# Attention and two gated layers on one core: side pieces stored one slot after their join, the last ones moved beside the fourth layer, and the third matrix's low parts on GpSimd

## The chip, the cores and the metric

The kernel runs on one core of a Trainium2 chip. The metric is the device time of one execution in microseconds. Five engines run their own queues in order and meet only at semaphores: TensorE (PE, with its weight loads as PEld), VectorE (DVE), ScalarE (ACT), GpSimd (POOL) and SyncE (SP), which here only issues DMAs. ACT issues DMAs too. An instruction that waits holds everything behind it on its engine's queue.

## What is computed

```python
def reference(**kwargs):
    attn_out = _attn_ref(q, k, v, w_pre, w_post)          # 4 batches, 12 heads, 448 positions, 64 per head
    x = attn_out.transpose(0, 2, 1, 3).reshape(1792, 768)
    x = ((x @ w1) * (x @ w2) @ w3) @ w_out                # moe:  768 -> 1024 -> 1024 -> 768
    h = np.maximum(x @ w_in, 0.0)                         # moe2: 768 -> 2048
    return h * h @ w_out2                                 # 2048 -> 768
```

Everything is float32. The change touches only what comes after the attention.

## The kernel before

**Numbers in two parts.** A float32 matrix is split into a high part (rounded by ACT, `high`, L120) and a low part (what is left, `rest`, L148), and each product is three matmuls, high by high, low by high and high by low (`mm3`, L56). PE therefore needs, for each weight piece, first `wh` and, from its third matmul on, `wl`. Some weights come from memory as eight-byte words. Such a piece is loaded by SP, folded by ACT (`fold`, L93), put together by DVE in two steps (the join, L104 and L106) and then split.

**Units and slots.** The class `Moe` lists units of work: `l1` (first layer), `p34` (the product w3 by w_out, made once, so that third and output matrix become one), `ly` (that product's layer, 12 slots for the first half of the tokens), `l3_quad` (the layer with w_in, seven block products `qh..A` to `qh..D` instead of eight, which need sums `Sh` of weight blocks), and `l4_part`. `run` goes over the units slot by slot. For each slot `stage` first writes the preparation of later pieces (load six ahead, fold four ahead, join and `high` three ahead, `rest` two ahead), and then the slot's matmuls and what becomes of their results. This program order is the order on every engine.

In the program, a `p34` slot has 24 matmuls of 384 columns, an `ly` slot 24 matmuls of 448 columns, a slot of a quad nine of 448, and an `l4` slot 24 of 448. An `ly` slot leaves one block of y. `yquad` (L891) evacuates it on ACT, rounds it, and, on every fourth slot (block B22), makes the differences T2, T3 and T4 on DVE, whose high parts ACT makes and whose low parts POOL makes (DVE for the last column).

**Side pieces.** The matrix w_in comes as eight-byte words too. It is put together ahead of its use in 32 side pieces, which are written back to the scratch tensor `wind` and read from there by the quads. `side(k)` (L967) handles at step k the join of piece k-2 (fold on ACT at L93, two DVE steps at L974 and L975), its store on ACT's queue (L978), and the load of piece k on SP (L981). The load reuses the buffer of piece k-2, so SP waits for that join. The condition at L671 says which slots have a step: both slots of each `p34` unit, one of two in the four `l1` units behind it, then all slots from `ly` on until 32 pieces are through. The last loads stand in the last `ly` slots, and the last two joins in the first two slots of the first quad.

**Low parts of the third matrix.** The pieces of `p34` carry a third field (L956). `stage` takes that as the sign to put their `rest` on DVE (L609). Other pieces' low parts are on POOL.

Of the kernel before, what the change touches and what calls it, by code (L numbers as in the profile page):

```python
# [26 lines left out]
PW = 512  # L27
# [10 lines left out]
def fused_kernel(ctx, tc, q, k, v, w_pre, w_post, w1, w2, w3t, wo, win, wo2, eye, out):  # L38
    nc = tc.nc
    PSUM = bass.MemoryType.PSUM  # L40

    def pool(stack, name, side="left", space=None):
        kw = {"space": space} if space is not None else {}
        return stack.enter_context(tc.tile_pool(name=name, bufs=1, side=side, reuse_waits="tile", **kw))
# [5 lines left out]
    wind = dram.tile([16, 128, DM], F, name="wind")  # L50
# [5 lines left out]
    def mm3(acc, terms, first=True, last=True, again=False):  # L56
        n = len(terms)
        for i, ((wh, wl), (xh, xl)) in enumerate(terms):
            for j, (w, x) in enumerate(((wh, xh), (wh, xl), (wl, xh))):
                nc.tensor.matmul(  # L60
                    acc, w, x, start=(first and i == 0 and j == 0), stop=(last and i == n - 1 and j == 2),
                    skip_group_check=again,
                )

    class Weights:


        def __init__(self, p, pre, wo, nraw, ny, nf, nhi, nlo):
            self.pre = pre
            self.p, self.wo, self.nraw, self.ny, self.nf, self.nhi, self.nlo = p, wo, nraw, ny, nf, nhi, nlo  # L70
            self.raw, self.yt, self.ft, self.out = {}, {}, {}, {}
# [461 lines left out]
    class Moe:  # L533
        def __init__(self, pre):
            self.w = Weights(None, pre, PW, 4, 2, 3, 8, 8)
            self.wp, self.pre = None, pre
            self.xy, self.late, self.acc, self.ready = {}, [[] for _ in range(8)], {}, set()
            self.units, self.wot = [], {}
            self.sides = 0
            for hf in range(2):  # L540
                if hf == 0:
                    l1 = [self.l1(hf, m, s) for m in range(6) for s in range(2)]
                else:
                    l1 = [self.l1_quad(j, s) for j in range(4) for s in range(2)]
                if hf == 0:

                    wop = [self.wo_piece(c, h) for c in range(8) for h in range(2)]
                    mixed, rest = l1[:4] + wop[:6], wop[6:]
                    for i in range(8):
                        mixed.append(l1[4 + i])  # L550
                        for _ in range(1 + (i % 4 == 3)):
                            mixed.append(rest.pop(0))
                    assert not rest
                    l1 = mixed
                self.units += l1
                ly = [self.ly(hf, n) for n in range(6)]
                if hf == 0:
                    self.p34_at = len(self.units)
                    self.units += [self.p34(m) for m in range(8)]
                    self.units += [self.l1(0, m, x) for m in (6, 7) for x in range(2)]  # L560
                self.turned = len(self.units)
                self.units += [self.ly(hf, n) for n in range(6)]
                for gr in range(4):
                    js = ((0, 1, 2), (3, 4), (5, 6, 7) if hf == 0 else (5, 6), () if hf == 0 else (7,))[gr]
                    self.units += [self.l3_quad(hf, j) for j in js]
                    es = [(0, 1), (2,), (3,), (4,), (5,)] if hf and gr == 3 else [(e,) for e in range(6)]
                    self.units += [self.l4_part(hf, gr, x) for x in es]
            kept = [u[2] if len(u) > 2 else None for u in self.units]
            self.units = [u[:2] for u in self.units]
            self.pieces = [s for ss, _ in self.units for s in ss]  # L570
            n = np.cumsum([0] + [len(ss) for ss, _ in self.units])
            self.at = [int(x) for x in n]
            self.keep = {
                self.at[i] + j: u[0][:, u[1] * j : u[1] * j + u[1]]
                for i, u in enumerate(kept) if u for j in range(len(self.units[i][0]))
            }
# [83 lines left out]
        def run(self, ps):  # L660
            self.ps = ps
            order = [None, None, (0, 1), None, (1, 1), None, (2, 1), None, (3, 1)]
            for i in range(10, len(self.units)):
                one = [(i, t) if self.units[i][1] else None for t in range(len(self.units[i][0]))]
                order += one[::-1] if i == self.turned else one
            for p, it in enumerate(order):
                def go():
                    i, t = it
                    ws = [self.w.out.get(self.at[i] + j) for j in range(len(self.units[i][0]))]
                    self.units[i][1](ws, t)  # L670
                    if i >= self.p34_at and (t or not self.p34_at + 8 <= i < self.p34_at + 12):  # L671
                        self.side(self.sides)
                        self.sides += 1

                self.stage(p + 5, go if it else None)

# [269 lines left out]
        def p34(self, m):  # L946
            def run(ws, t):
                acc = self.psum(f"p34_{m}_{t}")[:, :HC]
                mm3(acc, [(self.chunk(ws, c), self.wot[c, t]) for c in range(8)])
                o = self.tile(f"o34_{m}_{t}")[:, :HC]  # L950
                nc.scalar.activation(o, acc, AF.Copy)
                nc.scalar.dma_start(
                    w34d[3 * t : 3 * t + 3, :, m].rearrange("n p c -> p n c"), o.rearrange("p (n c) -> p n c", c=128)
                )

            return [(w3t[m, :, PW * i : PW * i + PW], True, None) for i in range(2)], run  # L956

        def ly(self, hf, n):
            def run(ws, t):
# [7 lines left out]
        def side(self, k):  # L967
            part = lambda x, i: x[i // 2, :, HC * (i % 2) : HC * (i % 2) + HC]
            if 0 <= k - 2 < 32:
                raw = self.w.raw["side", k - 2]  # L970
                f = self.tile(f"side{k - 2}")[:, :HC]
                fi = f.bitcast(I32)
                self.w.fold(raw[:, :, 1].bitcast(F), ("side", k - 2))
                nc.vector.tensor_scalar(fi, raw[:, :, 1], 3, None, ALU.logical_shift_left)  # L974
                nc.vector.scalar_tensor_tensor(  # L975
                    fi, raw[:, :, 0], 29, fi, ALU.logical_shift_right, ALU.bitwise_or
                )
                nc.scalar.dma_start(part(wind, k - 2), f)  # L978
            if 0 <= k < 32:
                t = self.w.raw["side", k] = self.ap.tile([128, HC, 2], I32, tag="sraw", name=f"sraw{k}", bufs=2)  # L980
                nc.sync.dma_start(t.rearrange("p n t -> p (n t)"), part(win, k).bitcast(I32))  # L981
# [152 lines left out]
```

## Time and profile before

| | |
|---|---|
| median of 3 runs | 1301.47 us (1301.25 to 1303.01) |
| the profiled execution's own time | 1300.55 us |
| its span, first to last instruction | 1298.4 us |
| granted TensorE clock, mean over the span | 0.996 |
| busy: PE, DVE, ACT, POOL | 97%, 69%, 58%, 45% of the span |

The profile has one row for a group of instructions or for one instruction, with its start, its duration and, in square brackets, how long its engine was idle before it and what ended that. PE's durations overlap, since matmuls are pipelined: what counts for it is the distance from one start to the next. Shares over the whole span are averages over stages with different limits, so the stretches of the stages around the change are read apart.

### The profile page before, as it was taken

What the parts mean: (1) busy time and instruction counts of PE and PEld (TensorE: products, weight loads), DVE (VectorE), ACT (ScalarE), POOL (GpSimd) and SP (SyncE); (2) the same over time, 40 slices, a digit from 0 to 9 for tenths busy, and PEclk for the clock granted to TensorE, in tenths of its full rate; (3) what the DMA queues carried; (4) which work ended last, traced back from release to release, by engine and by line L of the source; (5) the groups of instructions that cost most, each with busy time, mean ns of one, the idle gap of its engine ahead of it and who ended that gap; (6) DMA issues with size and microseconds to landing.
All of it is one profiled execution on the core that took longest, in us unless ns stands there. A gap on an engine that the chain in (4) does not pass through costs nothing. (4 is left out here: it accounts for less than half of the span.)

```text
span 1298.4 us, 23243 instructions
## 1 busy us (share of the span) xinstructions
PE 1258.7 (97%) x8398; PEld 1084.8 (84%) x8398; DVE 889.5 (69%) x1585; ACT 749.9 (58%) x1645; POOL 584.8 (45%) x617
## 2 busy tenths in 40 slices
PE   7999999999997999999998999999999999999998
PEld 3677777776775898899986999999999999999998
DVE  4889889788888866665466938599777337544543
ACT  5988889887987655455334655363444345452520
POOL 4354264245323612001344735565777457553621
PEclk9999999999999999999998999999999999999999
DMA  6566576566565667699544425165312121212312
GB/s 218 164 185 194 132 202 210 143 180 198 151 167 171 203 191 219 229 305 295 160 156 140 139 86 161 58 214 191 129 58 65 57 74 41 82 35 64 89 31 87
DMA packets 107462, 190.79 MB, mean 147 GB/s; under 512 B 21845, under 2 KB 73045, under 8 KB 106837
## 3 DMA queue, kind: packets, MB, share of 16 engines
q1 hardware_dynamic: 86928, 166.69, 42.5%
q10 hardware_dynamic: 20421, 22.63, 4.9%
q8 instruction: 66, 1.08, 0.3%
q14 instruction: 47, 0.39, 0.1%
HBM read 117.72 MB, written 33.03 MB: 116 GB/s over the span
## 5 line engine op out<-in xcount | busy, mean ns | idle before, releaser
L321 PE MATMUL sp<-r,kpre 120*120 120x448 f32 x360 | 158.6, 561 | 11.5 <-ACT p L335 6.6
L148 POOL TENSOR_TENSOR wl<-f,wh 128x384 fp32r<-128x384 f32 (+1 forms) x56 | 67.9, 1212 | 198.2 <-ACT wh L120 177.7
L335 ACT ACTIVATE p<-sp,nm 120x448 f32<-120x448 f32 x180 | 113.7, 643 | 48.4 <-DVE nm L327 48.2
L377 DVE SCALAR_TENSOR_TENSOR pl<-p,sm,ph 120x448 f16<-120x448 f32 (+3 forms) x270 | 138.0, 564 | 0.3 <-POOL ph L363 0.3
L327 DVE TENSOR_REDUCE nm<-sp 120x1 f32<-120x448 f32 x180 | 107.2, 617 | 40.9 <-PE sp L321 36.6
L386 PEld LDWEIGHTS <-ph 120*128 120x128 f16 x1260 | 92.9, 98 | 32.3 <-issue 23.8
L361 ACT ACTIVATE ph<-p,sm 120x448 f16<-120x448 f32 (+1 forms) x180 | 107.8, 664 | 17.2 <-DVE sm L355 13.5
L350 POOL TENSOR_SCALAR sm<-sm 120x2 f32<-120x2 f32 (+3 forms) x94 | 24.8, 264 | 204.1 <-ACT p L335 196.1
L148 POOL TENSOR_TENSOR wl<-Sh,wh 128x384 fp32r<-128x384 f32 x64 | 76.6, 1212 | 78.6 <-ACT wh L120 69.2
L386 PE MATMUL tp<-kwh,ph 120*128 120x120 f16 x630 | 106.1, 217 | 5.3 <-DVE p L402 2.2
L386 PE MATMUL tp<-kwh,pl 120*128 120x120 f16 x630 | 105.2, 216 | 0.0
L386 PE MATMUL tp<-kwl,ph 120*128 120x120 f16 x630 | 105.2, 216 | 0.0
L321 PEld LDWEIGHTS sp<-r,kpre 120*120 120x120 f32 x360 | 58.5, 183 | 55.3 <-issue 20.9
L295 PE MATMUL sc<-kt,qh 128*110 128x448 f32 (+1 forms) x192 | 98.2, 511 | 2.2 <-DVE kt L259 1.5
L306 ACT ACTIVATE s<-sc 110x448 f32<-110x448 f32 (+1 forms) x186 | 90.7, 560 | 6.1 <-PE sc L295 5.4
L120 ACT ACTIVATE wh<-f 128x512 fp32r<-128x512 f32 (+1 forms) x72 | 41.9, 582 | 72.6 <-DVE f L106 47.0
L438 PE MATMUL pv<-p,v 128*64 128x110 f32 (+1 forms) x1536 | 81.0, 262 | 0.6 <-ACT xs L448 0.6
L438 PEld LDWEIGHTS pv<-p,v 128*64 128x64 f32 x1536 | 74.1, 137 | 4.0 <-ACT xs L448 0.9
L400 DVE TENSOR_SCALAR p<-tp,iv 128x360 f32<-128x360 f32 x135 | 74.1, 576 | 1.3 <-PE tp L386 1.3
L148 POOL TENSOR_TENSOR wl<-quadh,wh 128x384 fp32r<-128x384 f32 x48 | 55.7, 1164 | 42.8 <-ACT wh L120 40.1
L148 POOL TENSOR_TENSOR wl<-raw,wh 128x512 fp32r<-128x512 f32 x48 | 63.1, 1326 | 23.4 <-ACT wh L120 19.1
L295 PE MATMUL sc<-kt,ql 128*110 128x448 f32 (+1 forms) x192 | 70.7, 368 | 0.0
(1980 smaller groups left out, 3884.8 us busy)
## 6 DMA issues: line engine op xcount, KB each, us to landing
r<-s SPq DMA_DIRECT2D x172, 210.0 KB
raw<-w SPq DMA_DIRECT2D x32, 384.0 KB
sraw<-win SPq DMA_DIRECT2D x32, 384.0 KB
quadh<-wind SPq DMA_DIRECT2D x32, 384.0 KB
raw<-wo SPq DMA_DIRECT2D x24, 512.0 KB
kraw<-k SPq DMA_DIRECT2D x24, 448.0 KB
raw<-w3t SPq DMA_DIRECT2D x16, 512.0 KB
qraw<-q SPq DMA_DIRECT2D x35, 220.0 KB
```

The costliest lines, as they stand in the source:

```text
L120: nc.scalar.activation(self.out[i][0], self.ft[i], AF.Copy)
L148: eng.tensor_tensor(self.out[i][1], self.ft.pop(i), f32(self.out[i][0]), ALU.subtract)
L295: nc.tensor.matmul(sc[:ic], t[:, hh * ic : hh * ic + ic], self.kt[b, h // 2][:, h % 2], start=(i == 0), stop=(i == 1))
L306: nc.scalar.activation(self.st[n][:ic, h], self.sc.pop((n, h))[:ic], AF.Copy)
L321: nc.tensor.matmul(t[:kk], self.kpre[:kk, :kk], self.rt.pop(g)[:kk], start=True, stop=True)
L327: nc.vector.tensor_reduce(nm[:kk], self.sp[g][:kk], AX.X, ALU.max, negate=True)
L335: nc.scalar.activation(p[:kk], self.sp.pop(g)[:kk], AF.Exp, bias=self.nm.pop(g)[:kk], accum_out=self.sm[g // 2][:kk, g % 2 : g % 2 + 1],)
L361: nc.scalar.activation(h[:, to], p[:, fr], AF.Copy, scale=sm)
L377: nc.vector.scalar_tensor_tensor(l[:, to], p[:, fr], sm, h[:, to], ALU.mult, ALU.subtract)
L386: nc.tensor.matmul(t[:, j], p[:, at : at + 128], w, start=(i == 0), stop=(i == 2))
L400: nc.vector.tensor_scalar(d, t[:, main], self.iv, None, ALU.mult)
L438: nc.tensor.matmul(t[64 * e : 64 * e + 64, x, :w], self.v[b][:, j, g], self.p2[n][:, j * NH + g, :w], start=(j == 0), stop=(j == JC - 1),)
```

## The change

It has three parts. `side(k)` now keeps the joined piece and stores piece k-3 instead of k-2, so a store is written into ACT's queue one step after its join. The steps are given by a set `free` of slots: the slots of `p34`, one of two in the four `l1` units and the first four `ly` units (28 steps, the same slots as before), then the six `l4` slots of the first group, and one slot of the second group for the last store. So the joins of pieces 26 to 31 and the loads of 28 to 31 leave the last four `ly` slots and the first quad. The pieces of `p34` lose their third field, so their 16 low parts go to POOL.

```diff
-            self.sides = 0
+            self.sides, self.step = {}, 0
...
+                if hf == 0:
+                    k = self.turned
+                    self.free = {(i, t) for i in range(self.p34_at, k + 4) for t in range(2)}
+                    self.free -= {(i, 0) for i in range(k - 4, k)}
+                    self.free |= {(k + 9 + e, 0) for e in range(6)}
+                    self.free |= {(k + 17, 0)}
...
-                    if i >= self.p34_at and (t or not self.p34_at + 8 <= i < self.p34_at + 12):
-                        self.side(self.sides)
-                        self.sides += 1
+                    if (i, t) in self.free:
+                        self.side(self.step)
+                        self.step += 1
...
-            return [(w3t[m, :, PW * i : PW * i + PW], True, None) for i in range(2)], run
+            return [(w3t[m, :, PW * i : PW * i + PW], True) for i in range(2)], run
...
-                nc.scalar.dma_start(part(wind, k - 2), f)
+                self.sides[k - 2] = f
+            if k - 3 in self.sides:
+                nc.scalar.dma_start(part(wind, k - 3), self.sides.pop(k - 3))
```

On ACT, around an `ly` slot, before. `sraw` is the folded side piece, `wh70` the high part of a weight piece three slots ahead, `y0B21raw` the evacuation of the slot's result:

```order
L933 ACTIVATE y0B21raw0_9148<-y0_1_0_9123 128x448 [waits PE_49]
L913 ACTIVATE y0_0h0_9040<-y0B21raw0_9148 128x448 [waits Activation_49]
L93 ACTIVATE sraw20_9071<-sraw20_9071 128x384 [waits DMAHW5_49]
L978 DMA wind_60<-side20_9152 128x384 [waits DVE_49]
L120 ACTIVATE wh70_9161<-raw70_9007 128x512 [waits DMAHW3_49,Pool_49]
```

The same place after:

```order
L938 ACTIVATE y0B21raw0_9147<-y0_1_0_9122 128x448 [waits PE_49]
L918 ACTIVATE y0_0h0_9039<-y0B21raw0_9147 128x448 [waits Activation_49]
L93 ACTIVATE sraw20_9070<-sraw20_9070 128x384 [waits DMAHW4_49]
L985 DMA wind_60<-side19_9109 128x384 [waits DVE_49]
L120 ACTIVATE wh70_9160<-raw70_9006 128x512 [waits DMAHW2_49,Pool_49]
```

Between the fold of piece 20 and the next high part stands now the store of piece 19, whose join was written one slot earlier, where the store of piece 20 stood.

On DVE, at the first `p34` slot, before. `wl40` and `wl41` are the low parts of its two weight pieces, `f41` and `f42` the joins of the second and third piece, `p0_5_1` a product of the first layer:

```order
L737 TENSOR_TENSOR p0_5_1_7965<-l1_0_5_1_1_7944,a0_5_1_7887 128x448 [waits PE_49]
L104 TENSOR_SCALAR f41_7972<-y41_7934 128x512
L106 SCALAR_TENSOR_TENSOR f41_7972<-raw41_7891,f41_7972 128x512 [waits DMAHW6_49,DVE_49]
L148 TENSOR_TENSOR wl40_7940<-f40_7936,wh40_7939 128x512 [waits Activation_49]
L104 TENSOR_SCALAR f42_7983<-y42_7970 128x512 [waits Activation_49]
L106 SCALAR_TENSOR_TENSOR f42_7983<-raw42_7900,f42_7983 128x512 [waits DMAHW0_49,DVE_49]
L148 TENSOR_TENSOR wl41_7976<-f41_7972,wh41_7975 128x512 [waits Activation_49]
```

The same place after:

```order
L742 TENSOR_TENSOR p0_5_1_7965<-l1_0_5_1_1_7944,a0_5_1_7887 128x448 [waits PE_49]
L104 TENSOR_SCALAR f41_7972<-y41_7934 128x512
L106 SCALAR_TENSOR_TENSOR f41_7972<-raw41_7891,f41_7972 128x512 [waits DMAHW6_49,DVE_49]
L104 TENSOR_SCALAR f42_7983<-y42_7970 128x512 [waits Activation_49]
L106 SCALAR_TENSOR_TENSOR f42_7983<-raw42_7900,f42_7983 128x512 [waits DMAHW0_49,DVE_49]
L104 TENSOR_SCALAR f43_7994<-y43_7981 128x512 [waits Activation_49,Pool_49]
```

The low parts are gone from DVE (they stand on POOL, behind nothing of this stage), and the join of `f43` now waits for POOL too, since it reuses the buffer that POOL's `wl40` reads.

On ACT, from the last `ly` slot into the first quad, before. `y0T42h` is the high part of T4, `s1h00` the evacuation of the quad's first product:

```order
L913 ACTIVATE y0T42h_9060<-y0T4raw2_9554 128x448 [waits DVE_49]
L93 ACTIVATE sraw29_9475<-sraw29_9475 128x384 [waits DMAHW6_49]
L978 DMA wind_60<-side29_9560 128x384 [waits DMAHW1_49,DVE_49]
L120 ACTIVATE wh79_9573<-quadh000_9255 128x384 [waits Pool_49]
L813 ACTIVATE s1h00_9587<-qh00A_9577 128x448 [waits PE_49]
L93 ACTIVATE sraw30_9515<-sraw30_9515 128x384 [waits DMAHW0_49,Activation_49]
L978 DMA wind_60<-side30_9589 128x384 [waits DMAHW5_49,DVE_49]
L120 ACTIVATE wh80_9596<-Sh003_9571 128x384 [waits Pool_49]
```

The same place after:

```order
L918 ACTIVATE y0T42h_9059<-y0T4raw2_9532 128x448 [waits DVE_49]
L120 ACTIVATE wh79_9544<-quadh000_9254 128x384 [waits Pool_49]
L818 ACTIVATE s1h00_9558<-qh00A_9548 128x448 [waits DMAHW4_49,PE_49]
L120 ACTIVATE wh80_9562<-Sh003_9542 128x384 [waits DVE_49,Pool_49]
L120 ACTIVATE wh81_9578<-Sh004_9560 128x384 [waits DVE_49,Pool_49]
```

The folds and stores of the side pieces are gone from this place. They stand in the `l4` slots, each behind the two evacuations of its slot.

## Rows read from the trace of the kernel before

**Rows 1.** Busy time of each engine in five stretches: `p34`, `ly`, first quad, second and third quad, `l4`.
```profile
core 0: us, PE busy (x) PEld busy (x) DVE busy (x) ACT busy (x) POOL busy (x), PEclk, DMA share, GB/s
534.12:602.90 68.78, 66.75 (x385) 66.42 (x384) 41.86 (x80) 33.93 (x62) 1.02 (x1) 1.00 0.87 279
...
631.70:697.10 65.40, 60.33 (x290) 55.01 (x289) 36.51 (x40) 25.26 (x49) 27.68 (x23) 0.97 0.43 135
697.10:716.00 18.90, 15.74 (x66) 12.70 (x65) 14.11 (x23) 9.61 (x21) 9.02 (x10) 0.91 0.50 171
716.00:741.50 25.50, 25.50 (x128) 23.64 (x127) 25.25 (x31) 16.66 (x34) 20.56 (x16) 1.00 0.29 94
741.50:770.30 28.80, 28.80 (x145) 27.00 (x145) 13.36 (x20) 13.67 (x28) 10.90 (x9) 1.00 0.41 138
```

**Rows 2.** Waits of PE over the span, after the attention: total us, times, longest.
```profile
PE y L60 <- POOL wl L148: 5.1, 4, 2.8
...
PE qh00A L60 <- ACT s1h L813: 2.2, 1, 2.2
...
PE p L60 <- DVE wl L148: 2.0, 1, 2.0
```

**Rows 3.** A piece of the chain that ended last: start, us, matmuls without a gap.
```profile
862.08 57.60 PE l L60 x288
```

**Rows 4.** One `ly` slot in order of time, all engines, and PE's first wait there.
```profile
654.63 1.50 DVE L916 TENSOR_TENSOR y0T4raw<-y0B21raw,y0T2raw 128x448 f32<-128x448 f32 x1
...
656.65 0.54 ACT L93 ACTIVATE sraw<-sraw 128x384 f32<-128x384 f32 x1
...
657.22 0.96 DVE L974 TENSOR_SCALAR side<-sraw 128x384 int32<-128x384 int32 x1 [1.09 <-ACT sraw L93]
...
657.93 1.41 POOL L148 TENSOR_TENSOR wl<-raw,wh 128x512 fp32r<-128x512 f32 x1
...
658.22 1.53 DVE L975 SCALAR_TENSOR_TENSOR side<-sraw,side 128x384 int32<-128x384 int32 x1
...
659.78 0.35 ACTq L978 DMA_DIRECT2D wind<-side  x1
...
660.23 0.63 ACT L120 ACTIVATE wh<-raw 128x512 fp32r<-128x512 f32 x1 [3.04 <-DVE side L975]
...
660.77 0.53 ACT L933 ACTIVATE y0B11raw<-y 128x448 f32<-128x448 f32 x1
...
664.54 0.47 PE L60 MATMUL y<-ab_0h,wl 128*128 128x448 f32 x1 [1.00 <-POOL wl L148]
```

**Rows 5.** Groups by line and form in 631 to 697, the `ly` stretch.
```profile
L120 ACT ACTIVATE wh<-raw 128x512 fp32r<-128x512 f32 x9 | 5.7, 632 | 27.7 <-DVE side L975 25.1 <-DVE Sh L144 2.5
```

**Rows 6.** PE after its longest wait, in order of time.
```profile
690.27 0.57 PE L60 MATMUL y<-ab_0h,wl 128*128 128x448 f32 x1
690.65 0.57 PE L60 MATMUL y<-ab_0h,wh 128*128 128x448 f32 x1
```

**Rows 7.** The first quad's beginning: DVE, ACT and PE in order of time.
```profile
697.85 1.26 DVE L975 SCALAR_TENSOR_TENSOR side<-sraw,side 128x384 int32<-128x384 int32 x1
699.03 0.61 DVE L916 TENSOR_TENSOR y0T2raw<-y,y0T1raw 128x448 f32<-128x448 f32 x1
...
705.73 0.53 ACT L813 ACTIVATE s1h<-qh00A 128x448 f32<-128x448 f32 x1
...
706.31 0.47 PE L60 MATMUL qh00A<-y_0h,wh 128*128 128x448 f32 x1 [2.16 <-ACT s1h L813]
```

**Rows 8.** The first `p34` slot: PE, DVE and ACT in order of time.
```profile
535.93 0.68 DVE L148 TENSOR_TENSOR wl<-f,wh 128x512 fp32r<-128x512 f32 x1
...
536.10 0.63 ACT L120 ACTIVATE wh<-f 128x512 fp32r<-128x512 f32 x1 [2.10 <-DVE f L106]
```

**Rows 9.** Groups by line and form in 536 to 603, the `p34` stretch.
```profile
L148 DVE TENSOR_TENSOR wl<-f,wh 128x512 fp32r<-128x512 f32 x16 | 11.1, 691 | 3.9 <-ACT wh L120 3.5
...
L975 DVE SCALAR_TENSOR_TENSOR side<-sraw,side 128x384 int32<-128x384 int32 x13 | 7.3, 559 | 0.5
...
L974 DVE TENSOR_SCALAR side<-sraw 128x384 int32<-128x384 int32 x13 | 4.7, 361 | 21.7 <-ACT sraw L93 21.7
```

**Rows 10.** DVE at the end of the first `l4` group, in order of time.
```profile
773.99 0.62 DVE L789 TENSOR_TENSOR u2h<-qh03B,s1h 128x448 f32<-128x448 f32 x1 [14.29 <-PE qh03B L60]
```

More of the change, by code (lines that the diff above doesn't have):

```diff
@@ L555, in __init__ @@
                 self.units += l1
-                ly = [self.ly(hf, n) for n in range(6)]
                 if hf == 0:
```

## The prediction

> **What bounds the kernel now.** I read the busy shares first: PE 97% of 1298.4 us. So only PE's idle or slowed time can be won, and I looked for that: the windows by stage [rows 1] and the list of what PE waits for [rows 2]. Only three places around the change show any. From the second quad to the end of the `l4` stretch PE is busy for all of its time, and a piece of the last chain shows what an undisturbed stretch is: 288 matmuls of 448 columns in 57.60 us, 0.200 us each [rows 3]. With that price each place has a floor.
>
> `ly`: 12 slots of 24 matmuls are 288, so 57.6 us. It takes 65.4 [rows 1]: 7.8 lost.
>
> First quad: seven products of nine matmuls are 63, so 12.6 us. It takes 18.9 [rows 1]: 6.3 lost.
>
> `p34`: one wait of 2.0 us for a low part [rows 2]. The rest, 66.8 us for 384 matmuls of 384 columns, is 0.174 each.
>
> The time at stake is 7.8 + 6.3 + 2.0 = 16.1 us, 1.2% of the kernel.
>
> PE's waits in `ly` come to only 5.1 us [rows 2], less than the 7.8. The rest is pace: after the wait of 2.8 us PE's matmuls start 0.38 apart instead of 0.20 [rows 6], and the granted clock of the two stretches is 0.97 and 0.91 of full speed, 1.00 elsewhere [rows 1]. So a wait there costs itself and a slow piece behind it, and I count with the stretches' whole excess.
>
> **Why `ly` loses.** [Rows 4] is one slot. ACT folds a side piece at 656.65. DVE's join takes 0.96 and 1.53 us and ends about 659.75. ACT's store of that very piece goes at 659.78, and only then can ACT run the next `wh`, at 660.23, after 3.04 us of idleness. POOL makes the low part from it, and PE waits 1.00 us at 664.54. The group shows that it recurs: nine such `wh` have 27.7 us of idle ACT ahead of them, 25.1 of it put down to the join's second step [rows 5], about 3 us per slot. ACT is neither full (25.3 us of work in 65.4) nor slow. It stands behind a store that waits for a join written just before.
>
> **Part 1, stores one slot later.** It removes no instruction. In ACT's order the store behind the fold of piece 20 is now that of piece 19, whose join DVE did a slot, some 5 us, earlier. ACT's idle 3 us per slot go. Its slot then has 25.3/12 = 2.1 us of work and a store's 0.35, against a PE slot of 4.8. DVE has 36.5 us and POOL 27.7 for a stretch of 57.6 [rows 1]: no engine is the next bound. Late next are the slots of block B22, where DVE makes three differences of 1.5 us before the join [rows 4]. In those DVE's part of a slot comes near the 4.8, and the three slots behind have slack to catch up. Side effect: the joined piece is held a slot longer, but DVE has no other step on it.
>
> **Part 2, the last six side pieces moved.** It takes from the last four `ly` slots and the first quad the work that makes the quad start late. [Rows 7]: DVE still does a join (697.85, 1.26 us) when the quad's stretch has begun, and T2 comes after it, at 699.03. T2, T3 and T4, then their high parts on ACT, then `s1h` stand in one line, and `s1h` runs at 705.73, with PE waiting 2.16 us until it is done. Without the joins DVE goes at once into five differences of about 0.6 us, 3.0 us; ACT then needs one high part, one `wh` and `s1h` at 0.5 to 0.6 each, 1.6 more. That is 4.6 us after `ly`'s end. PE wants it after three products, 3 x 1.8 = 5.4. The slack is 0.8 us, so the 6.3 go nearly whole. Because DVE is then full (25.25 of 25.5 us in the next two quads [rows 1]), I leave 0.4 of loss: the first reuse of a result bank must find its sums done at 7.2 us.
>
> Where the six joins go, in the `l4` stretch, DVE works 13.4 us of 28.8 and ACT 13.7 [rows 1], and DVE stands idle for 14.29 us in one piece at its end [rows 10]. Six joins are 6 x 0.92 = 5.5 us on DVE alone (0.361 + 0.559 [rows 9]) and 6 x 2.49 = 15 us beside POOL [rows 4]; ACT gets 6 x (0.54 + 0.35) = 5.3 us. Either fits into the 15.4 us that DVE has free, and ACT's into its 15.1. On SP the loads of pieces 28 to 31 now wait for joins with the loads of the next quads queued behind them; those have slots to spare, and the moved pieces themselves are read only by the last two quads of this half, behind two other quads and a second `l4` group. I cost it at 0; if the cover were missing, PE would wait once for a sum or an evacuation behind a join beside POOL, 2.5 us.
>
> **Part 3, low parts of the third matrix on POOL.** On DVE 16 low parts of 691 ns go, 11.1 us of 41.9 [rows 9, 1]. POOL, with 1.02 us of work in this stretch [rows 1], gets 16 of up to 1.41 us [rows 4], 22.6 of 68.8. DVE is not the bound there: per slot it has 41.86/16 = 2.6 us against PE's 4.17. So this can win only the wait of 2.0 us. There the first low part was queued on DVE behind a join and ran at 535.93 for 0.68, while its input was ready before 534.00, when ACT went idle [rows 8]. On POOL it ends by 534.00 + 1.41 = 535.4, 1.2 us sooner. But the second piece's high part starts as before at 536.10 and ends at 536.73. On DVE its low part was early enough; on POOL it ends at 538.14. Before, PE reached it 12 x 0.174 = 2.1 us after the first, at 536.61 + 2.09 = 538.7. So PE's gain ends at 538.7 - 538.1 = **0.6 us**. Bounds: 0, if POOL's operation there is as slowed as DVE's beside it (1.53 for 0.559 [rows 4, 9]), and 2.0, the whole wait. I take 0.6, since 1.41 was itself measured beside a DVE operation.
>
> New wait: the join of the fourth piece waits on DVE until POOL has read the first piece's buffer. Queued behind it are DVE's other joins and then a `wh` on ACT; but that low part ends two joins before. Cost 0, up to 0.5.
>
> What is left on DVE, 1.92 us per slot, will be slower beside POOL. [Rows 4] against [rows 9] shows it: 0.96 for 0.361, 1.53 for 0.559, so about 0.6 to 1.0 more per step that meets POOL. POOL runs at most 1.41 of the 4.17 us, so I add at most 1.41: 3.3 of 4.17. Hidden.
>
> The Trainium skill (SBUF — State Buffer, section Who interferes with whom) speaks against this part: a DVE instruction with two inputs in SBUF and a GpSimd instruction that reads SBUF exclude each other for the whole instruction, so work moved from one to the other would still hold the first. The trace agrees as to `ly` (1.53 beside POOL, 0.559 without). By the rule DVE would be blocked for 16 x 1.41 = 22.6 us of `p34`, an estimate: 41.9 - 11.1 + 22.6 = 53.4 of 68.8, still hidden; but POOL's second low part could be held by a DVE step as long as the 0.6 to be won, and the sum would be 13.7, or 1287.8.
>
> **Sum.** 7.8 (`ly`) + 6.3 - 0.4 (first quad) + 0.6 (`p34`) = 14.3 us. From the profiled execution's 1300.55 that is 1286.25. The median shown is 0.92 higher than that execution, so on its scale **1287.2**. All 16.1 gained would give 1285.4.
>
> **Rivals.**
>
> *Half of it.* The quad's first differences still come late, because T2 to T4 need the last `ly` block and `s1h` follows with only 0.8 us of slack, and a wait there is followed by slow matmuls. Then its 6.3 stay: 14.3 - 5.9 = 8.4 won, so 1293.1. The same size comes if the B22 slots stay late: 2 us, itself and the slow piece behind it, in each of three columns is 6, so 8.3 won and 1293.2. For: the PE waits of [rows 2] are few and costly, so one that stays keeps much. Against: 3 us of ACT's idleness per slot go, more than either place lacks.
>
> *Slower.* POOL's low parts slow all of DVE's work in `p34`, not only what they meet. Place: the joins there, ahead of ACT's `wh` and PE. Price: 1.92 us x 1.53/0.559 = 5.26 per slot against 4.17, 1.09 x 16 = 17.4 us lost. With 13.7 won in `ly` and quad: 1300.55 - 13.7 + 17.4 + 0.9 = 1305.2. It decides from the point where a slot's DVE work passes 4.17 us, a factor of 2.2 on all of it. Against: POOL is free for two thirds of each slot.
>
> *It does not do what it says.* The store is not what holds `wh`: the next thing in ACT's line, the evacuation or the buffer that `wh` shares with POOL, is as late. Then the 3 us turn up behind another name and the time stays at about 1301. For: in [rows 5] 2.5 us have another cause already. Against: 25.1 of 27.7 have this one.
>
> **How the numbers follow.** About 0.2% (2.6 us) is what a measurement of this kernel can tell from no change. Forecast 1287.2: 0.72, spread from 1285.4 to about 1290 by the bounds of `p34` (0 to 2.0), the quad's 0.4 and the `l4` cover (2.5). Half: 0.17, at 1293, itself spread by a microsecond or so. Same: 0.05. Slower: 0.05. Better than 1285: 0.01. The range from 1285.0 to 1293.5 leaves out some 0.15. Faster 0.90, same 0.05, slower 0.05.
>
> **What would show it.** Right: an `ly` stretch of about 57.6 us and a first quad of about 12.8, both at granted clock 1.00; no ACT `wh` idle behind the side join; PE's list of waits without POOL's `wl` of 2.8 and without `s1h`; in `p34` PE's one wait now for POOL, some 1.4 us in all; joins in `p34` longer than 361 and 559 ns while that stretch keeps its 67 to 69 us; the 14.29 us gap of DVE in `l4` shorter. Wrong: new PE waits inside `p34` behind a join; waits in `ly` every fourth slot; a wait in the first quad behind T4's high part or behind a sum of the first result bank; or PE idle at the end of `l4` or in the last quads behind a late side piece.

## The result, and the profile after

The changed kernel takes 1286.7 us (median of 4 runs, 1284.18 to 1289.6) beside 1302.24 us of the kernel before (4 runs): a ratio of 0.988, 95% interval 0.9856 to 0.9905. The prediction was 1287.2. The profiled execution's span fell from 1298.4 to 1284.0 us, 14.4 us where the sum had 14.3; the medians fell by 15.5, by the interval of the ratio 12.4 to 18.8.

The windows of the kernel after by stage, in the columns of [rows 1]: `p34`, `ly`, first quad, second and third quad, first `l4` group.

```profile
533.88:602.61 68.73, 67.11 (x385) 66.42 (x385) 47.43 (x65) 34.98 (x64) 24.50 (x18) 1.00 0.87 284
...
631.41:689.01 57.60, 57.60 (x289) 53.99 (x288) 34.54 (x35) 23.71 (x46) 31.02 (x25) 1.00 0.45 144
689.01:701.70 12.69, 12.69 (x65) 11.73 (x63) 10.87 (x16) 7.98 (x17) 7.24 (x7) 1.00 0.20 64
701.70:726.92 25.22, 25.22 (x128) 23.60 (x126) 24.93 (x29) 16.43 (x34) 20.12 (x16) 1.00 0.30 89
726.92:755.72 28.80, 28.80 (x146) 26.99 (x144) 19.61 (x28) 15.98 (x33) 11.96 (x9) 1.00 0.70 231
```

`ly` is at its floor of 57.6 us and the first quad at 12.69, PE busy for all of both, at full granted clock. Cut at the same places (first matmul to first matmul), the stages of before were 68.86, 65.36, 18.82, 25.36 and 28.80 us. So `ly` gave 7.76, the first quad 6.13, the next two 0.14 and `p34` 0.13; 0.24 lies ahead of `p34`, which no part of the change touches. The sum is 14.40.

PE's waits after the attention, the answer to [rows 2]:

```profile
PE p L60 <- POOL wl L148: 1.6, 2, 0.9
PE l L60 <- POOL wl L148: 0.4, 1, 0.4
PE l L60 <- ACT wh L120: 0.4, 1, 0.4
```

The waits of `ly` and of the quad are gone. In `p34` one wait of 2.0 us became two of 0.8 and 0.85.

Parts of two `ly` slots, DVE, POOL and ACT in order of time (start, duration), the answer to [rows 4]:

```profile
655.80 0.98 DVE L979 TENSOR_SCALAR side<-sraw 128x384 int32<-128x384 int32 x1 [1.08 <-ACT sraw L93]
...
656.53 1.41 POOL L148 TENSOR_TENSOR wl<-raw,wh 128x512 fp32r<-128x512 f32 x1
...
656.83 1.53 DVE L980 SCALAR_TENSOR_TENSOR side<-sraw,side 128x384 int32<-128x384 int32 x1
...
661.95 0.33 ACTq L985 DMA_DIRECT2D wind<-side  x1
662.21 0.54 ACT L93 ACTIVATE sraw<-sraw 128x384 f32<-128x384 f32 x1
...
662.64 0.61 ACT L120 ACTIVATE wh<-raw 128x512 fp32r<-128x512 f32 x1
662.78 0.98 DVE L979 TENSOR_SCALAR side<-sraw 128x384 int32<-128x384 int32 x1 [1.09 <-ACT sraw L93]
```

The join is as slow as before, 0.98 and 1.53 us. But fold and `wh` now follow each other on ACT without a pause, and `wh` has begun at 662.64 before the join of the piece folded just ahead of it begins at 662.78. The answer to [rows 5], where nine `wh` had 27.7 us of idle ACT ahead of them:

```profile
L120 ACT ACTIVATE wh<-raw 128x512 fp32r<-128x512 f32 x8 | 4.9, 618 | 1.1 <-DVE side L980 1.1
```

And the first quad's beginning, the answer to [rows 7]:

```profile
689.21 0.62 DVE L921 TENSOR_TENSOR y0T2raw<-y,y0T1raw 128x448 f32<-128x448 f32 x1 [8.12 <-PE y L60]
...
693.17 0.53 ACT L818 ACTIVATE s1h<-qh00A 128x448 f32<-128x448 f32 x1
...
694.41 0.36 PE L60 MATMUL qh00A<-y_0h,wh 128*128 128x448 f32 x1
695.20 0.61 DVE L794 TENSOR_TENSOR u2h<-qh00B,s1h 128x448 f32<-128x448 f32 x1
```

DVE starts T2 at once, 0.20 us after `ly`'s end. `s1h` is done at 693.70, and PE, at 694.41, no longer waits for it.

### The profile page after: what moved, and what is told of

It reads as the page before. It is cut to its first block, busy times and chain, and to the rows that moved or that the text cites. A ratio compares the mean times of both kernels' runs of the same rounds, so it can differ in the third digit from the quotient of the medians.

```text
span 1284.0 us, 23281 instructions
## 1 busy us (share of the span) xinstructions
PE 1252.7 (98%) x8398; PEld 1081.6 (84%) x8398; DVE 901.2 (70%) x1569; ACT 750.3 (58%) x1645; POOL 609.2 (47%) x633
## 4 chain that ended last, share of the span: by engine, by line
PE 82%; DVE 5%; issue 4%; DMA 4%; POOL 2%; ACT 2%; SPq 0%; ACTq 0%; DVEq 0%; POOLq 0%
PE l L60 22%; PE y L60 9%; PE sp L321 8%; PE p L60 5%; PE pv L438 5%; PE tp L386 5%; PE sc L295 4%; DMA r<-s 3%; DVE pl L377 2%; POOL wl L148 1%; DVE nm L327 1%; DMA kraw<-k 1%; DVE p L400 1%; ACT ph L361 1%; ACT p L335 1%
## 5 line engine op out<-in xcount | busy, mean ns | idle before, releaser
L148 POOL TENSOR_TENSOR wl<-f,wh 128x512 fp32r<-128x512 f32 (+1 forms) x72 | 90.8, 1262 | 174.6 <-ACT wh L120 151.3
L350 POOL TENSOR_SCALAR sm<-sm 120x2 f32<-120x2 f32 (+3 forms) x94 | 25.1, 267 | 203.7 <-ACT p L335 202.5
L104 DVE TENSOR_SCALAR f<-y 128x384 int32<-128x384 int32 (+1 forms) x88 | 65.8, 748 | 15.4 <-ACT y L93 10.8
```

The lines of the kernel that those rows point to most:

```text
L148: eng.tensor_tensor(self.out[i][1], self.ft.pop(i), f32(self.out[i][0]), ALU.subtract)
```

## The experiments

The theory: in `ly`, ACT stood behind the store of a piece that was just being joined (A); the first quad was late because joins stood ahead of T2. The first rival (B): the joins, stretched beside POOL, are too much for DVE in `ly`, wherever the store stands. Stage times below are from each kernel's profile, cut as above (the 70.4 of two kernels is taken up in the last section); medians and ratios are against runs of the kernel before on the same chip.

| kernel | p34 | ly | first quad | quads 2, 3 | l4 | median | ratio, 95% |
|---|---|---|---|---|---|---|---|
| before | 68.86 | 65.36 | 18.82 | 25.36 | 28.80 | 1300.7 to 1302.2 | |
| changed | 68.73 | 57.60 | 12.69 | 25.22 | 28.80 | 1286.7 | 0.9856 to 0.9905 |
| store_later | 70.42 | 57.60 | 15.66 | 25.95 | 28.80 | 1291.93 | 0.9915 to 0.9945 |
| moved_only | 68.38 | 65.94 | 12.66 | 25.21 | 28.80 | 1293.32 | 0.9925 to 0.9955 |
| pool_only | 68.70 | 65.64 | 19.12 | 25.33 | 28.80 | 1300.93 | 0.9985 to 1.0011 |
| no_pool | 68.80 | 57.61 | 12.65 | 25.21 | 28.80 | 1286.8 | 0.9878 to 0.9909 |
| sp_store | 70.43 | 57.60 | 15.18 | 25.99 | 28.80 | 1289.96 | 0.9882 to 0.9933 |
| last_four | 68.86 | 57.60 | 16.26 | 25.20 | 28.80 | 1290.05 | 0.9885 to 0.9934 |
| beside_quads | 68.68 | 57.60 | 12.68 | 30.95 | 32.61 | 1295.66 | 0.9931 to 0.9966 |
| side_twice | 68.85 | 57.60 | 12.69 | 25.20 | 28.80 | 1286.27 | 0.9857 to 0.9902 |
| all_twice | 77.39 | 57.60 | 12.67 | 25.21 | 28.80 | 1295.14 | 0.9930 to 0.9972 |
| product_later | 68.42 | 57.60 | 12.67 | 25.21 | 28.80 | 1285.36 | 0.9858 to 0.9896 |

**Part 1 alone** (store_later), made from the kernel before:

```diff
...
-                nc.scalar.dma_start(part(wind, k - 2), f)
+                self.sides[k - 2] = f
+            if k - 3 in self.sides:
+                nc.scalar.dma_start(part(wind, k - 3), self.sides.pop(k - 3))
```

> Only part 1: stores one step later, side pieces still in all ly slots and the first quad, third matrix's low parts on DVE. Theory A (ACT stood behind the store of a piece just being joined): the ly stretch falls from 65.4 to 57.6-58.5 us and no high part waits for the join's second step there. The first quad keeps part of its loss, since two joins still stand ahead of T2: by the rows of before, T4's high part, a fold, a store, wh and s1h in line give s1h at about 8 us after ly's end where PE wants it at 5.4, so 15 to 17 us instead of 18.8. In all 1290 to 1293 us beside 1302.2. Rival B (ly is slow because the joins, stretched beside POOL, are too much DVE work there, wherever the store stands): ly stays at 63 us or more, 1299 to 1302 us.

`ly` is 57.60 and the quad 15.66, both in A's ranges, and B falls, since `ly` has as many joins as before. But what keeps the quad late is not `s1h` behind joins ahead of T2, as I had argued: T2 starts 0.27 us after `ly`'s end (691.64), and `s1h` ends 5.14 after it, before PE wants it. Its DVE rows and PE's wait:

```profile
696.06 0.35 DVE L974 TENSOR_SCALAR side<-sraw 128x384 int32<-128x384 int32 x1
696.45 1.40 DVE L975 SCALAR_TENSOR_TENSOR side<-sraw,side 128x384 int32<-128x384 int32 x1
...
698.24 0.34 DVE L974 TENSOR_SCALAR side<-sraw 128x384 int32<-128x384 int32 x1
698.62 0.56 DVE L975 SCALAR_TENSOR_TENSOR side<-sraw,side 128x384 int32<-128x384 int32 x1
...
700.37 0.61 DVE L789 TENSOR_TENSOR u2h<-qh00B,s1h 128x448 f32<-128x448 f32 x1
...
701.13 0.44 PE L60 MATMUL qh00B<-y0T30h,wh 128*128 128x448 f32 x1 [1.96 <-DVE u2h L789]
```

Two joins stand on DVE between T4 and `u2h`, the sum that frees the quad's second result bank, and PE waits 1.96 us for it. It is the place at which the prediction left 0.4 us.

**Parts 2 and 3 without 1** (moved_only): the changed kernel with the store of piece k-2 right behind its join again. Against what the expectation says, the third matrix's low parts are on POOL in this kernel.

> Only part 2: the last six side pieces beside the fourth layer, each store still right behind its own join, low parts on DVE. Theory A: the first eight ly slots keep their loss (8/12 of 7.8, about 5 us: ly at 62 to 63), the last four and the first quad lose nothing (quad 12.7): about 1293 to 1294 us. Rival B: taking joins away is what heals, ly at 60 or less and 1288 to 1291 us.

The quad is healed (12.66), as A had it, but `ly` is not: 65.94 us, as much as before, though its last four slots have no side step. Neither number for `ly` came, A's 62 to 63 or B's 60 or less. The total of 1293.32 lies in A's range all the same: that is luck, since A counted from 1302.2, the kernel before took 1300.7 on this chip, and the five stages of the profile give 6.2 us where A had 8.2 to 9.2. The group of `wh` in `ly` says why:

```profile
L120 ACT ACTIVATE wh<-raw 128x512 fp32r<-128x512 f32 x9 | 5.7, 632 | 27.9 <-DVE side L980 25.4 <-DVE Sh L144 2.5
```

It is the same nine `wh` with the same idle time as in [rows 5]. A `wh` is made three slots before its use, so the stores of the last `ly` slots hold up the quad's pieces and no matmul of `ly`. I had shared the loss out over the slots in which PE waits, not over those in which ACT works for them. The next kernel puts that to the test.

**The first eight ly slots cleared, the last four not** (last_four): stores right behind their joins on ACT, low parts on DVE. The edit of the slots, against the changed kernel:

```diff
-                    self.free = {(i, t) for i in range(self.p34_at, k + 4) for t in range(2)}
+                    self.free = {(i, t) for i in range(self.p34_at, k) for t in range(2)}
+                    self.free |= {(k + 4 + i, t) for i in range(2) for t in range(2)}
...
-                    self.free |= {(k + 17, 0)}
+                    self.free |= {(k + 17 + e, 0) for e in range(5)}
```

> The kernel before (stores right behind their joins on ACT, third matrix's low parts on DVE) with other slots for the side steps: none in the first eight ly slots, four in the last four, the other twelve beside the fourth layer's first and second group. Theory A with the lead of three slots (a stall counts where the high part is made, three slots before its use, so only the first nine ly slots matter): ly 57.6 to 58.5 us, the first quad 14 to 17 us, since a join still stands ahead of T2. Rival (each ly slot with a store loses its share where it stands): 4/12 of 7.8 lost in the last four slots, ly at 60 to 60.5.

`ly` is 57.60 with four undelayed stores in it. The lead of three slots is right. Here the quad waits for `s1h` again, with the join ahead of T2:

```profile
688.09 1.25 DVE L981 SCALAR_TENSOR_TENSOR side<-sraw,side 128x384 int32<-128x384 int32 x1
689.39 0.63 DVE L922 TENSOR_TENSOR y0T2raw<-y,y0T1raw 128x448 f32<-128x448 f32 x1
...
695.17 0.34 ACTq L984 DMA_DIRECT2D wind<-side  x1
695.56 0.52 ACT L120 ACTIVATE wh<-quadh 128x384 fp32r<-128x384 f32 x1 [1.57 <-DVE side L981]
695.99 0.53 ACT L819 ACTIVATE s1h<-qh00A 128x448 f32<-128x448 f32 x1
...
696.57 0.65 PE L60 MATMUL qh00A<-y_0h,wh 128*128 128x448 f32 x1 [1.80 <-ACT s1h L819]
```

T2 begins 0.20 us after `ly`'s end at 689.19, as in the changed kernel. But `s1h` ends at 696.52, 7.3 us after it, where the changed kernel needs 4.7: on ACT it stands behind a store and a `wh`, and the store waited 1.57 us for a join that began after T4. So most of what I had put down to the join ahead of T2 (3.66 of the 6.22 us that the quad had above 12.6) is the same thing as in `ly`, a store that waits on ACT.

**The store on another queue** (sp_store): the kernel before with `nc.sync.dma_start(part(wind, k - 2), f)` in place of the store on ScalarE's queue.

> The kernel before with one edit: the store of a side piece, still right behind its join, is issued from SyncE's queue instead of ScalarE's. Theory A (the place of the wait in ACT's queue is all): ly 57.6 to 58.5 us, no high part there waits for the join, although the joins are where they were; the first quad like the one with the store a step later, 15 to 17; 1290 to 1293 us. Rival B (the joins' work on DVE beside POOL): ly at 63 or more. Rival C (the wait only moves to SP, and weights behind it come late): ly or p34 with new waits of PE behind late weights, 1296 or more.

`ly` is 57.60 and the quad 15.18, as with the store one step later. The joins and their order are those of before; only the queue that waits is another. In `ly` no `wh` has idle ACT ahead of it, and SP waits for the joins' second step instead, 38.8 us in nine waits:

```profile
L120 ACT ACTIVATE wh<-raw 128x512 fp32r<-128x512 f32 x8 | 4.9, 616 | 0.0
...
SPq L978 <- DVE side L975: 38.8, 9, 6.9
```

This shows A most directly, and SP's own wait cost PE nothing that shows.

**Part 3 alone, and the change without it** (pool_only, no_pool).

> Only part 3: the third matrix's low parts on GpSimd. Theory A: p34 0.1 to 0.6 us shorter, ly still 65.4 and the first quad 18.8, so 1301.6 to 1302.2 us, not to be told from before. Rival (DVE was short of time in p34 and handed its lateness on): ly shorter by 2 us or more, below 1300. The slower rival of the prediction: p34 longer by 15 us, 1317.

> Parts 1 and 2 without part 3. Theory A: ly 57.6, first quad 12.7, p34 as before with one wait of 2.0 us for DVE (0.1 to 0.3 us longer than with part 3): 1287 us, within 0.5 of the changed kernel. Rival (part 3 carries part of the gain): 1289 us or more.

Part 3 alone is not to be told from before (ratio 0.9998), and without it the change is as fast (1286.8). Its 0.1 us in `p34` stays below what the times can show.

**The six steps beside the second and third quad** (beside_quads):

```diff
-                    self.free |= {(k + 9 + e, 0) for e in range(6)}
-                    self.free |= {(k + 17, 0)}
+                    self.free |= {(k + 7 + e // 3, 2 * (e % 3)) for e in range(6)}
+                    self.free |= {(k + 9, 0)}
```

> The changed kernel with the six moved side steps beside the second and third quad instead of the fourth layer. Theory A (a place is free only where DVE has time): DVE works 24.9 of 25.2 us there, six joins add 5.5 us at least and up to 15, so the two quads take 29 to 35 us instead of 25.2, 1290 to 1297 us in all. Rival (any slot outside ly will do, PE has enough ahead): 25.2 to 26, 1287.

The two quads take 30.95 us, as A had it, and the `l4` group behind them 32.61, which I had not expected. PE's waits there (of the 3.0 us, 2.6 lie here):

```profile
PE l L60 <- ACT wh L120: 3.0, 2, 2.6
PE qh02B L60 <- DVE u2h L794: 1.9, 1, 1.9
```

DVE ran without a gap from 702.00 to 728.63, and its lateness came out first at the sums of the second bank. The first weights of `l4` were late by another link, SP's queue. There the loads of the moved side pieces wait for joins, and the loads of `l4`'s weights stand behind them:

```profile
709.37 15.10 SPq L988 DMA_DIRECT2D sraw<-win  x4
724.57 13.74 SPq L77 DMA_DIRECT2D raw<-wo  x6
...
730.16 0.66 ACT L93 ACTIVATE y<-raw 128x512 f32<-128x512 f32 x1 [3.79 <-DMA raw<-wo]
```

The first of those weight loads goes 33.6 us after the first quad's beginning, in the changed kernel 18.1, and ACT stood idle for it. Behind the wait of 2.6 us the granted clock fell too: its mean over the `l4` group is 0.90, in the changed kernel 1.00. On the same chip side_twice, which leaves the steps beside `l4`, took 1286.27: the place of six joins decides 9 us.

**DVE's cover in p34** (side_twice, all_twice): the two instructions of each side join there are issued twice; in the second kernel also those of the joins of the third matrix's pieces.

```diff
+                for _ in range(2 if k < 16 else 1):
-                nc.vector.tensor_scalar(fi, raw[:, :, 1], 3, None, ALU.logical_shift_left)
+                    nc.vector.tensor_scalar(fi, raw[:, :, 1], 3, None, ALU.logical_shift_left)
...
-                for part in range(2):
-                    w.join(s + 3, part)
+                twice = self.at[self.p34_at] <= s + 3 < self.at[self.p34_at + 8]
+                for part in (0, 1, 0, 1) if twice else (0, 1):
+                    w.join(s + 3, part, twice)
...
```

> The changed kernel, in which DVE does the two steps of each side join in p34 twice. Theory A (DVE is covered in p34 up to 4.17 us a slot): 47.4/16 = 2.96 us of work a slot, plus 0.92, is 3.9: hidden, p34 68.5 to 69.2 us, 1286 to 1288. The prediction's slower rival (DVE in p34 is already at its limit beside POOL): p34 longer by 0.92 x 14 = 13 us.

> As the kernel with the side joins done twice in p34, and the joins of the third matrix's own pieces twice as well. Theory A (the bound is DVE's work per slot against 4.17 us of PE): 57.1/16 = 3.57 us measured with the side joins twice, plus 1.18 to 2.0 (a join of 0.42 and 0.76 alone, up to 1.26 and 0.76 beside POOL), is 4.75 to 5.6 a slot: over the bound by 0.6 to 1.4, less the first slots' lead of three pieces, p34 77 to 90 us instead of 68.7 and 1295 to 1308 us in all. Rival (DVE and POOL run apart in time enough that the added work finds room): under 72 us, 1287 to 1290.

The windows of `p34` in the two:

```profile
534.52:603.37 68.85, 67.19 (x385) 66.50 (x385) 57.13 (x89) 35.81 (x64) 24.71 (x18) 1.00 0.85 270
...
536.36:613.75 77.39, 69.67 (x385) 66.14 (x386) 73.61 (x117) 33.51 (x63) 22.53 (x18) 1.00 0.73 233
```

57.1 us of DVE's work are hidden, 73.6 are not: `p34` then takes 77.39 us, of which DVE works 95%. That is the lowest end of what A said, because little of the second dose met POOL (the first step of those joins took 539 ns on average). So DVE can become the bound of `p34`, as the slower rival had it, though here by doubled work and not by POOL. At 47.4 us in the changed kernel it is at least 9.7 us short of that; where between 57.1 and 73.6 it begins is not shown.

**The product one slot later** (product_later), aimed at what `p34` still loses:

```diff
+                    def mul():
-                    nc.vector.tensor_tensor(p, acc, self.xy["a", m, t], ALU.mult)
-                    self.split_late(ab, p)
+                        nc.vector.tensor_tensor(p, acc, self.xy["a", m, t], ALU.mult)
+                        self.split_late(ab, p)
+                    if (hf, m) == (0, 5):
+                        self.late[0].append(mul)
+                    else:
+                        mul()
```

> The changed kernel with the last two products of the first layer ahead of p34 written one slot later, so that on DVE the join of p34's second piece stands ahead of the product that waits for PE. Theory A (p34's second wait comes from that join's place): the join ends about 0.7 us sooner, PE's second wait (0.85 us) goes, the first (0.8) may stay: p34 67.6 to 68.2 us instead of 68.7, in all 0.5 to 1.1 us less than the changed kernel, too little to tell by the time. Rival (the join waits for something else, its fold or its load): 68.7.

68.42 us, 0.31 less than the changed kernel, where A had 0.5 to 1.1; the median of 1285.36 can't be told from 1286.7. And the wait that was to go, the second, stayed at 0.85; the first shrank, from 0.8 to 0.5. The join did start sooner, but beside POOL's first low part:

```profile
533.28 1.45 DVE L104 TENSOR_SCALAR f<-y 128x512 int32<-128x512 int32 x1
...
533.17 1.28 POOL L148 TENSOR_TENSOR wl<-f,wh 128x512 fp32r<-128x512 f32 x1 [4.80 <-ACT wh L120]
...
537.71 0.45 PE L60 MATMUL p<-wo_0h,wl 128*128 128x384 f32 x1 [0.85 <-POOL wl L148]
```

Counted from `p34`'s first matmul its first step started 0.98 us sooner, but took 1.45 us, in the changed kernel 0.77, and so gave back 0.68. POOL's low parts came 0.3 us sooner, the first as well as the second, so PE reached the second that much sooner too.

## Why the prediction was right, point by point

**What bounds the kernel.** The floors held to 0.1 us: 57.60 for `ly`, 12.69 against 12.6 for the first quad. Counting the stretches' whole excess and not PE's waits alone was right too: 5.1 us of waits in `ly` gave back 7.76. That the sum is as close as 14.3 to 14.40 is in part luck: the 0.47 that part 3 did not bring is made up by 0.23 more in the first quad and 0.38 that no term had (0.14 in the next two quads, 0.24 ahead of `p34`).

**Part 1.** Shown by store_later and sp_store: the store's place on ACT alone takes `ly` to its floor. "Late next are the slots of block B22" cost nothing; PE has no wait there.

**Part 2.** Right in size: 5.9 us predicted for the first quad, 6.13 measured; of the 0.4 left as loss 0.09 came. `s1h` ended 4.69 us after `ly` (4.6 predicted), 0.71 before PE wanted it. The parts overlap: part 1 alone takes the first quad from 18.82 to 15.66, part 2 (with 3) to 12.66 (moved_only). What was late there was told only half right: with the stores waiting on ACT it is `s1h` behind a store (last_four), and without that it is `u2h` behind two joins (store_later), not T2.

In the `l4` stretch DVE's work rose by 6.1 us, 13.54 to 19.61. Five joins fall into it (4.6 us at 0.92 each, 12.5 at 2.49); the sixth begins just behind it. The stretch stayed at 28.80, so the cover held. DVE's longest idle piece there, 14.29 us in [rows 10], is split up; between the joins there are at most 3.85 us now:

```profile
752.56 0.36 DVE L979 TENSOR_SCALAR side<-sraw 128x384 int32<-128x384 int32 x1 [3.84 <-ACT sraw L93]
...
757.36 0.36 DVE L979 TENSOR_SCALAR side<-sraw 128x384 int32<-128x384 int32 x1 [3.85 <-ACT sraw L93]
```

**Part 3** is the term that was mis-sized: 0.6 predicted, 0.13 measured. The step that failed is "the second piece's high part starts as before". The rows of the first `p34` slot after, answering [rows 8]:

```profile
533.76 1.34 POOL L148 TENSOR_TENSOR wl<-f,wh 128x512 fp32r<-128x512 f32 x1 [5.06 <-ACT wh L120]
...
534.61 0.77 DVE L104 TENSOR_SCALAR f<-y 128x512 int32<-128x512 int32 x1
...
536.21 0.63 ACT L120 ACTIVATE wh<-f 128x512 fp32r<-128x512 f32 x1 [1.96 <-DVE f L106]
...
538.37 0.44 PE L60 MATMUL p<-wo_0h,wl 128*128 128x384 f32 x1 [0.85 <-POOL wl L148]
```

Counted from `p34`'s first matmul, that high part starts 2.33 us in, before 1.98. The join ahead of it was held by POOL's first low part, 0.77 us for a step that takes 0.42, and that 0.35 is most of the missing gain. I had let POOL be slowed by DVE there and not DVE by POOL, though the prediction says so of the steady slots. The sentence on the Trainium skill (SBUF — State Buffer, section Who interferes with whom) had the loss nearly right, since by its estimate the gain of 0.6 was lost, but not the hold: it let a DVE step hold POOL's second low part, and here POOL's first low part held a DVE step, one with a single input, which the rule as cited there does not cover.

DVE's work per slot was 47.43/16 = 2.96 us, under the 3.3 that I allowed. One sign that the prediction named did not come: the side joins in `p34` did not get longer (360 and 559 ns, before 361 and 559). What did was the first step of the third matrix's own joins (last section). Of PE's waits there one of some 1.4 us was said, and two of 1.6 together came. Nor is 0.13 a fixed size: with the same low parts on POOL `p34` took 68.70 us in pool_only and 68.38 in moved_only, 0.16 and 0.48 less than before.

**Rivals.** Half of it came to pass only where half of the change was made (store_later 1291.93, moved_only 1293.32; 1293.1 was said). The slower one needs over 9.7 us more of DVE's time in `p34` than the changed kernel has (side_twice). "It does not do what it says" fell with the 27.7 us that became 1.1.

## What to carry to other kernels

Here a DMA that ACT issued waited on ACT's queue for its data, and everything behind it waited too, 25.1 us of idle ACT and 7.8 us of PE: place a store behind the work that its producer needs time for, or on a queue with nothing urgent behind it. When sharing out such a loss, go by the slot in which the waiting engine works, not by that in which the result is missed; here they are three slots apart. Moved work is free only where the engine that takes it has time and where the loads that move with it hold up no urgent ones on their queue: beside `l4` six joins cost nothing, beside the quads 9 us.

## What the runs showed of the hardware that was not expected

**DVE's time for the same instructions depends on when they meet POOL.** DVE's groups in `p34`, pool_only first, then the changed kernel; both have the low parts on POOL:

```profile
L104 DVE TENSOR_SCALAR f<-y 128x512 int32<-128x512 int32 x15 | 7.9, 524 | 1.1 <-ACT y L93 1.1
```

```profile
L104 DVE TENSOR_SCALAR f<-y 128x512 int32<-128x512 int32 x15 | 18.9, 1261 | 1.1 <-ACT y L93 1.1
```

The stretch's DVE total is 33.82 us in the one and 47.43 in the other. With the store one step later ACT makes `wh` sooner, so POOL's low part starts just ahead of DVE's next join; in pool_only it starts behind both of that join's steps (at 573.28, the second step ending at 573.19). That it is the store and not the moved pieces shows in moved_only, which has the store at its old place and 33.42 us. After:

```profile
571.76 1.39 POOL L148 TENSOR_TENSOR wl<-f,wh 128x512 fp32r<-128x512 f32 x1 [2.77 <-ACT wh L120]
571.92 1.52 DVE L104 TENSOR_SCALAR f<-y 128x512 int32<-128x512 int32 x1
...
573.47 0.69 DVE L106 SCALAR_TENSOR_TENSOR f<-raw,f 128x512 int32<-128x512 int32 x1
```

The DVE step ends 0.29 us after POOL's, as if it had waited for it; the next, which meets no POOL, takes its usual 0.69. It is hidden here, but it is 13.6 us of DVE that no instruction count shows.

**The same wait has two prices.** Five kernels have `p34`'s wait of about 2.0 us for DVE's low part. Three have the stretch at 68.80 to 68.86 us, two (store_later, sp_store) at 70.4, with the same work. The stretches 534.8 to 540 and 540 to 545 of store_later, in the columns of [rows 1]:

```profile
534.80:540.00 5.20, 3.16 (x15) 2.84 (x15) 4.88 (x10) 2.73 (x5) 0.00 (x0) 0.89 0.58 197
540.00:545.00 5.00, 5.00 (x25) 5.00 (x24) 2.49 (x6) 1.58 (x4) 0.00 (x0) 0.78 0.98 332
```

The granted clock has a mean of 0.89 and 0.78 of the full 2.4 GHz there, so a part of the time ran at 1.2, and 25 matmuls fall into the second stretch, 31 into the same piece of the kernel before, where the clock stays at 1.00 behind the same wait. The first quad has such a pair too: with one wait of 1.96 us its mean clock is 1.00 (store_later), with one of 1.80 it is 0.90 (last_four). None of the seven profiles with the low parts on POOL, where PE's single waits in `p34` are at most 0.9 us, has a granted clock under 1.00 in `p34`. What decides between the two prices is open.
